# Query denominators in PSUM, another order of the query steps, and projections with the stationary tokens in two halves

## The chip, the core and the metric

The kernel runs on one core of a Trainium2 chip. A core has a matrix engine (TensorE, PE in the profile; its weight loads are listed apart as PEld), VectorE (DVE), ScalarE (ACT), GpSimd (POOL) and SyncE (SP), which issues the transfers. Each works through its own queue in order, and semaphores make one wait for another. SBUF is the working memory; PSUM, eight banks of 512 fp32 per partition, takes what TensorE writes. The metric is the device time of one execution in microseconds. The change is read as faster or slower where it differs from the time before by more than 2%.

## What is computed

Linear attention with a product of two small projections as feature map, and an MLP with a piecewise quadratic activation on its output.

```python
# batch, heads, sequence, head_dim = 4, 4, 1088, 32; r = 8; d_ff = 2048
def phi(x):
    a = np.einsum('rd,bhsd->bhsr', S1, x)
    b = np.einsum('rd,bhsd->bhsr', S2, x)
    return np.einsum('bhsi,bhsj->bhsij', a, b).reshape(*x.shape[:-1], r * r)
q_p, k_p = (phi(q), phi(k))
kv = np.einsum('bhsf,bhsd->bhfd', k_p, v)
z = np.sum(k_p, axis=2)
num = np.einsum('bhsf,bhfd->bhsd', q_p, kv)
den = np.einsum('bhsf,bhf->bhs', q_p, z)[..., None] + 1e-06
x = (num / den)            # then 4352 tokens of 4 * 32 = 128 values
h = x @ w_in               # 128 -> 2048
g = np.where(h >= 1, h, np.where(h <= -1, 0.0, (h + 1) ** 2 / 4))
out = g @ w_out            # 2048 -> 128
```

## The kernel before

A batch has nine tiles of 128 tokens, which are handled as three groups (`groups`) of three. For the keys of a batch, `features` multiplies each tile with the small matrix `s_sb` (the 128 tokens stationary, 64 columns moving; line 223), ScalarE copies one factor out of PSUM (line 227), and VectorE forms the 64 products per head (`kp`, line 229). `k_sums` then sums over all tokens in two PSUM banks (`kv`, line 255), and `projections` makes from the sums a third set of eight columns per head, so that a query tile, multiplied with the 96 columns of `proj`, also yields what its denominator needs.

For the queries of batches 1 to 3, a group goes through `q_steps_over`, four steps: `f` (`q_feat_over`: the projection `abc`, line 398; the copy `a_q`, 402; the products `ac`, 405; their sum, 406; 1e-6 added, 407; the reciprocal, 408; `a_q` times it, 409; the features `qp`, 411), `t` twice (`q_turn_over`: transposes `tp` and a copy), and `x` (`q_out`: the two matmuls of `xt`, line 436, each with 64 stationary columns and the output on one half of the partitions, and `place`, which writes the chunk's `x_hi` and `x_lo`). Batch 0 uses an older form of these steps, in `front` and in `q_steps`.

The MLP runs in 144 units: a chunk of 512 tokens (256 in the last) by 128 columns of d_ff. `up(u)` makes `h{u}` with three fp32r matmuls (high and low parts; lines 486 to 488), ScalarE and VectorE apply the activation (500, 501, 504, 505, or 507), GpSimd makes the low part `g_lo` (508), and `down` adds three matmuls into the chunk's `acc` (522 to 524), four units later. The first units of the first two chunks use whole fp32 (520) instead.

After every `up`, `advance` takes one step of the attention from a list: the string `FS` for batch 0, and `SS` for batches 1 to 3, where a digit and a letter name a query group and its step, and `k` is the next step of the next batch's keys. So the steps of all batches are done by about unit 62. The program is written in that order; a scheduler then fixes each engine's queue from it, so a step that is moved in the string can move other instructions too. Tiles come from pools, PSUM from one pool of eight banks.

Of the kernel before, what the change touches and what calls it, by code (L numbers as in the profile page):

```python
# [8 lines left out]
F32 = mybir.dt.float32  # L9
# [5 lines left out]
ALU = mybir.AluOpType  # L15
PSUM = bass.MemoryType.PSUM

P = 128
# [6 lines left out]
FIRST = 32  # L25
HI_ACT = (0.5, 0.35)
FS = "2t 2t 2n 2x s k k k k k k k"
SS = "0f k k 0t 0t 1f k 0x 1t k 1t 2f k 1x k 2t 2t k 2x"


def word_as_float(bits):
# [6 lines left out]
def tile_kernel(ctx: ExitStack, tc: tile.TileContext, qT, kT, v, S, w_in, w_out, outT):  # L38
    nc = tc.nc
    B, _, NTL, _ = qT.shape  # L40
    H, D, R = 4, 32, 8
# [8 lines left out]
    cst = ctx.enter_context(tc.tile_pool(name="cst", bufs=1))  # L50
    ld = ctx.enter_context(tc.tile_pool(name="ld", bufs=2))
    wk = ctx.enter_context(tc.tile_pool(name="wk", bufs=2))
# [4 lines left out]
    def bank(name):  # L57
        return ps.tile([P, 512], F32, tag="ps", name=name)
# [6 lines left out]
    for h in range(2):  # L65
# [5 lines left out]
                            axis=mybir.AxisListType.XY, op=ALU.add)  # L71
# [114 lines left out]
    s_sb = cst.tile([P, S.shape[1]], F32, name="s_sb")  # L186
# [27 lines left out]
    kv_sb = {}  # L214
    kv_part = {}


    def features(x_sb, grp, b, what, outs):

        n = len(grp)  # L220
        ab = bank(f"ab_{what}{b}_{grp[0]}")
        for i, t in enumerate(grp):
            nc.tensor.matmul(ab[:, i * 64 : (i + 1) * 64], lhsT=x_sb[:, t], rhs=s_sb, start=True, stop=True)
        a_sb = wk.tile([P, 3 * H, R], F32, tag="a_sb", name=f"a_{what}{b}_{grp[0]}", bufs=3)
        m = n * H
        abv = ab[:, : n * 64].rearrange("p (m c) -> p m c", c=2 * R)
        nc.scalar.copy(a_sb[:, :m], abv[:, :, :R])  # L227
        yield
        nc.vector.tensor_tensor(  # L229
            out=outs.rearrange("p t (h i j) -> p (t h) i j", h=H, i=R),  # L230
            in0=a_sb[:, :m].unsqueeze(3).broadcast_to([P, m, R, R]),
            in1=abv[:, :, R:].unsqueeze(2).broadcast_to([P, m, R, R]),
            op=ALU.mult,
        )
        yield
# [3 lines left out]
    def k_feat(b, g):  # L239
        if b not in batch:  # L240
            batch[b] = load_batch(b)
        if b not in kp_of:
            kp_of[b] = wk.tile([P, NTL, H * F], F32, tag="kw", name=f"kp{b}", bufs=1)
        grp = groups[g]
        yield from features(batch[b][0], grp, b, "k", kp_of[b][:, grp[0] : grp[-1] + 1])
# [52 lines left out]
    proj = {}  # L298
# [35 lines left out]
    def q_feat(b, g):  # L334
        grp = groups[g]
        qp_of[b, g] = wk.tile([P, 3, H * F], F32, tag="qp", name=f"qp{b}_{g}")
        yield from features(batch[b][2], grp, b, "q", qp_of[b, g][:, : len(grp)])
# [52 lines left out]
    def q_feat_over(b, g):  # L390

        grp = groups[g]
        n = len(grp)
        m = n * H
        q_sb = batch[b][2]
        abc = bank(f"abc{b}_{g}")
        for i, t in enumerate(grp):
            nc.tensor.matmul(abc[:, i * 96 : (i + 1) * 96], lhsT=q_sb[:, t], start=True, stop=True,  # L398
                             rhs=proj[b].rearrange("p h w r -> p (h w r)"))
        v3 = abc[:, : n * 96].rearrange("p (m c) -> p m c", c=3 * R)  # L400
        a_sb = wk.tile([P, 3 * H, R], F32, tag="a_sb", name=f"a_q{b}_{g}", bufs=3)
        nc.scalar.copy(a_sb[:, :m], v3[:, :, :R])
        ac = wk.tile([P, 3 * H, R], F32, tag="ac", name=f"ac{b}_{g}")
        den = wk.tile([P, 3 * H], F32, tag="dn", name=f"den{b}_{g}")
        nc.vector.tensor_tensor(out=ac[:, :m], in0=a_sb[:, :m], in1=v3[:, :, 2 * R :], op=ALU.mult)
        nc.vector.tensor_reduce(out=den[:, :m], in_=ac[:, :m], axis=mybir.AxisListType.X, op=ALU.add)
        nc.vector.tensor_scalar(out=den[:, :m], in0=den[:, :m], scalar1=1e-6, scalar2=None, op0=ALU.add)
        nc.vector.reciprocal(out=den[:, :m], in_=den[:, :m])
        nc.vector.tensor_tensor(out=a_sb[:, :m], in0=a_sb[:, :m], in1=den[:, :m].unsqueeze(2).broadcast_to([P, m, R]), op=ALU.mult)
        qp_of[b, g] = wk.tile([P, 3, H * F], F32, tag="qp", name=f"qp{b}_{g}")  # L410
        nc.vector.tensor_tensor(
            out=qp_of[b, g][:, :n].rearrange("p t (h i j) -> p (t h) i j", h=H, i=R),
            in0=a_sb[:, :m].unsqueeze(3).broadcast_to([P, m, R, R]),
            in1=v3[:, :, R : 2 * R].unsqueeze(2).broadcast_to([P, m, R, R]),
            op=ALU.mult,
        )
# [23 lines left out]
    def q_steps_over(b, g):  # L440
        q_feat_over(b, g)
        yield
        for p in range(2):
            q_turn_over(b, g, p)
            yield
        q_out(b, g)
        yield
# [128 lines left out]
    def merged(b, kb, seq):  # L576

        q = [(q_steps_over if b else q_steps)(b, g) for g in range(len(groups))]
        k = k_steps(kb) if kb < B else iter(())
        for e in seq.split():  # L580
            if e == "s":
                repeat_s2()
            elif e == "k":
                next(k, None)
                if kb >= B:
                    continue
            else:
                g = int(e[0])
                next(q[g])
                if e[1] == "x":  # L590
                    yield b * SEQ + min(SEQ, (g + 1) * 3 * P)
                    continue
            yield 0

    def steps():
        yield from merged(0, 1, FS)
        for b in range(1, B):
            yield from merged(b, b + 1, SS)

# [13 lines left out]
    for u in range(len(units)):  # L613
        c0, n, j = units[u]
        while todo and todo[0][0] <= j:
            _, make, c = todo.pop(0)
# [66 lines left out]
```

## Time and profile before

| | us |
|---|---|
| three runs | 287.23, 292.83, 371.11; median 292.83 |
| the profiled execution, device time | 287.16 |
| its span, first to last instruction | 285.3 |
| busy in the span: PE, DVE, ACT, POOL | 266.1, 218.5, 211.1, 190.6 |
| share of TensorE in the chain that ended last | 73% |

The rows have engine, line, operation, output and inputs, shape, count, then busy time and mean duration of one, and after the next bar how long the engine had idled before them and on whom. A row of the timeline starts with start and duration in us; neighbours of one kind are merged into one row with a count. Matmuls are pipelined, so the duration of one is longer than the time it keeps the array: what counts is the distance to the next start. An fp32 matmul leaves two records.

### The profile page before, as it was taken

The page shows a single profiled execution, that of the slowest core. Times are in us where ns is not written, and L with a number is a line of the kernel's source. Part 1 is how long each engine was busy: PE and PEld are TensorE (multiplying, and loading weights), DVE is VectorE, ACT ScalarE, POOL GpSimd, SP SyncE. Part 2 cuts the span into 40 slices and gives each one's busy share as a digit, 9 for nine tenths or more (in the row PEclk, how much of TensorE's full clock was granted, in tenths as well). Part 3 has the DMA queues.
Part 4 walks back from the last instruction along what each step waited for, and adds up shares of the span by engine and source line. Part 5 has one row for each costly group of instructions (what it writes and reads, how often), then busy time and mean ns, then how long its engine had stood idle before and what let it go on. Part 6 is the DMA issues. An engine that isn't in the chain of part 4 may idle for free.

```text
span 285.3 us, 4114 instructions
## 1 busy us (share of the span) xinstructions
PE 266.1 (93%) x1325; PEld 208.1 (73%) x1325; DVE 218.5 (77%) x387; ACT 211.1 (74%) x437; POOL 190.6 (67%) x171
## 2 busy tenths in 40 slices
PE   8876869999979999999995999999999999999994
PEld 5764747766749778778854777888888888888883
DVE  3547963969995789878875987788978778767774
ACT  2263845857557797957774677999999998989993
POOL 2071967067495565755573466799999989987892
PEclk9995659999999999999997999999999999999999
DMA  6999000220000100000000000010000000000001
GB/s 195 359 417 377 3 1 1 85 85 0 2 0 13 73 0 37 37 5 0 0 2 37 0 0 0 2 38 1 2 38 0 0 37 3 0 37 2 1 0 55
DMA packets 4772, 13.89 MB, mean 49 GB/s; under 512 B 528, under 2 KB 1296, under 8 KB 4752
## 3 DMA queue, kind: packets, MB, share of 16 engines
q1 hardware_dynamic: 4752, 13.64, 13.1%
q8 instruction: 10, 0.16, 0.2%
q14 instruction: 10, 0.08, 0.1%
HBM read 11.41 MB, written 2.23 MB: 48 GB/s over the span
## 4 chain that ended last, share of the span: by engine, by line
PE 73%; DVE 13%; ACT 5%; POOL 2%; DMA 2%; issue 2%; SPq 1%; DVEq 0%; ACTq 0%; POOLq 0%
PE h L486 10%; PE h L487 10%; PE h L488 10%; PE acc L524 9%; PE acc L522 8%; PE acc L523 8%; PE acc L520 5%; PE kv L255 4%; DMA v_sb<-in_v 2%; PE tp L425 2%; DVE s L505 2%; PE xt L436 2%; DVE g_hi L504 1%; PE abc L398 1%; ACT s L501 1%
## 5 line engine op out<-in xcount | busy, mean ns | idle before, releaser
L508 POOL TENSOR_TENSOR g_lo<-s,g_hi 128x512 fp32r<-128x512 f32 (+1 forms) x126 | 153.7, 1243 | 50.0 <-DVE s L505 23.7
L500 ACT ACTIVATE s<-h 128x512 f32<-128x512 f32 (+1 forms) x130 | 73.1, 573 | 28.8 <-PE h L488 27.0
L505 DVE SCALAR_TENSOR_TENSOR s<-h,s 128x512 f32<-128x512 f32 (+1 forms) x130 | 82.3, 653 | 7.3 <-ACT s L501 5.5
L501 ACT ACTIVATE s<-s 128x512 f32<-128x512 f32 (+1 forms) x130 | 76.7, 610 | 0.9
L504 DVE SCALAR_TENSOR_TENSOR g_hi<-h,s 128x512 fp32r<-128x512 f32 (+1 forms) x83 | 53.3, 648 | 27.3 <-ACT s L501 17.7
L486 PE MATMUL h<-x_hi,wi_hi 128*128 128x512 f32 (+1 forms) x144 | 61.0, 423 | 0.4 <-ACT x_hi L386 0.4
L487 PE MATMUL h<-x_lo,wi_hi 128*128 128x512 f32 (+1 forms) x144 | 56.0, 390 | 0.0
L488 PE MATMUL h<-x_hi,wi_lo 128*128 128x512 f32 (+1 forms) x144 | 55.6, 389 | 0.0
L524 PE MATMUL acc<-g_lo,wo_hi 128*128 128x512 f32 (+1 forms) x130 | 50.8, 396 | 1.8 <-POOL g_lo L508 1.1
L522 PE MATMUL acc<-g_hi,wo_lo 128*128 128x512 f32 (+1 forms) x130 | 50.4, 389 | 0.2 <-DVE g_hi L504 0.2
L523 PE MATMUL acc<-g_hi,wo_hi 128*128 128x512 f32 (+1 forms) x130 | 49.5, 381 | 0.0
L507 ACT CAST g_hi<-s 128x512 fp32r<-128x512 f32 (+1 forms) x47 | 28.3, 603 | 7.7 <-DVE s L505 7.5
L486 PEld LDWEIGHTS h<-x_hi,wi_hi 128*128 128x128 f32 x144 | 28.0, 195 | 7.9 <-issue 1.3
L488 PEld LDWEIGHTS h<-x_hi,wi_lo 128*128 128x128 f32 x144 | 27.7, 192 | 5.8
L487 PEld LDWEIGHTS h<-x_lo,wi_hi 128*128 128x128 f32 x144 | 28.0, 194 | 4.5 <-issue 0.2
L524 PEld LDWEIGHTS acc<-g_lo,wo_hi 128*128 128x128 f32 x130 | 24.4, 189 | 8.5 <-POOL g_lo L508 3.1
L522 PEld LDWEIGHTS acc<-g_hi,wo_lo 128*128 128x128 f32 x130 | 24.7, 190 | 6.1 <-issue 1.2
L130 POOL TENSOR_TENSOR loww<-loww,hcw 128x512 f32<-128x512 f32 x8 | 10.2, 1277 | 27.2 <-DVE hcw L105 26.8
L523 PEld LDWEIGHTS acc<-g_hi,wo_hi 128*128 128x128 f32 x130 | 24.5, 189 | 4.3
L255 PEld LDWEIGHTS kv<-v_sb,kp 128*128 128x128 f32 x108 | 14.4, 191 | 2.2 <-issue 1.0
L520 PE MATMUL acc<-s,wo 128*128 128x512 f32 x28 | 15.2, 664 | 0.8 <-DVE s L495 0.8
L229 DVE TENSOR_TENSOR kp<-a_k,ab_k 128x768 f32<-128x768 f32 x12 | 11.1, 943 | 4.4 <-ACT a_k L227 4.3
(96 smaller groups left out, 301.4 us busy)
## 6 DMA issues: line engine op xcount, KB each, us to landing
v_sb<-in_v SPq DMA_DIRECT2D x4, 594.0 KB, 8.5
raw_i<-in_w_in SPq DMA_DIRECT2D x4, 512.0 KB, 8.5
raw_o<-in_w_out SPq DMA_DIRECT2D x4, 512.0 KB, 7.6
outT<-o SPq DMA_DIRECT2D x8, 256.0 KB, 2.0
k_sb<-in_kT SPq DMA_DIRECT2D x3, 576.0 KB, 8.4
q_sb<-in_qT SPq DMA_DIRECT2D x3, 576.0 KB, 4.7
k_sb<-in_kT SPq DMA_DIRECT2D x3, 192.0 KB, 2.7
q_sb<-in_qT SPq DMA_DIRECT2D x1, 384.0 KB, 7.2
```

The source lines that it names most:

```text
L486: nc.tensor.matmul(h[:, :n], lhsT=wi_hi[:, fj], rhs=x_hi[:, :n], start=True, stop=False)
L487: nc.tensor.matmul(h[:, :n], lhsT=wi_hi[:, fj], rhs=x_lo[:, :n], start=False, stop=False)
L488: nc.tensor.matmul(h[:, :n], lhsT=wi_lo[:, fj], rhs=x_hi[:, :n], start=False, stop=True)
L500: nc.scalar.activation(s[:, :n], h[:, :n], AF.Relu, bias=0.5, scale=0.5)
L501: nc.scalar.activation(s[:, :n], s[:, :n], AF.Square)
L504: nc.vector.scalar_tensor_tensor(out=g_hi[:, :n], in0=h[:, :n], scalar=1.0, in1=s[:, :n], op0=ALU.max, op1=ALU.min)
L505: nc.vector.scalar_tensor_tensor(out=s[:, :n], in0=h[:, :n], scalar=1.0, in1=s[:, :n], op0=ALU.max, op1=ALU.min)
L508: (nc.vector if u >= len(units) - 4 else nc.gpsimd).tensor_tensor(out=g_lo[:, :n], in0=s[:, :n], in1=g_hi[:, :n].bitcast(F32), op=ALU.subt ...
L520: nc.tensor.matmul(acc[:, :n], lhsT=wo_32[:, fj], rhs=g_hi[:, :n], start=(j == 0), stop=False)
L522: nc.tensor.matmul(acc[:, :n], lhsT=wo_lo[:, fj], rhs=g_hi[:, :n], start=(j == 0), stop=False)
L523: nc.tensor.matmul(acc[:, :n], lhsT=wo_hi[:, fj], rhs=g_hi[:, :n], start=False, stop=False)
L524: nc.tensor.matmul(acc[:, :n], lhsT=wo_hi[:, fj], rhs=g_lo[:, :n], start=False, stop=(j == NJ - 1))
```

## The change

It has three parts. In `q_feat_over` the denominator is kept in twelve unused columns of the group's own PSUM bank `abc`; the products go into one of two fixed tiles `terms`, which hold 1e-6 as a ninth value, so the sum over nine replaces the sum over eight and the separate addition. The key projections and the query projections of batches 1 to 3 load the 128 stationary tokens as two halves of 64, each with its output on one half of the partitions: two matmuls in place of one. And the string `SS` is another.

```diff
-SS = "0f k k 0t 0t 1f k 0x 1t k 1t 2f k 1x k 2t 2t k 2x"
+SS = "0f k 1f k 0t k 0t k 2f 0x k 1t 1t k 1x k 2t 2t 2x"
...
+    terms = [cst.tile([P, 3 * H, R + 1], F32, name=f"terms{i}") for i in range(2)]
+    for t in terms:
+        nc.gpsimd.memset(t[:, :, R:], 1e-6)
...
         for i, t in enumerate(grp):
-            nc.tensor.matmul(ab[:, i * 64 : (i + 1) * 64], lhsT=x_sb[:, t], rhs=s_sb, start=True, stop=True)
+            for c in (slice(0, 64), slice(64, P)) if b else (slice(0, P),):
+                nc.tensor.matmul(ab[c, i * 64 : (i + 1) * 64], lhsT=x_sb[:, t, c], rhs=s_sb, start=True, stop=True)
...
         for i, t in enumerate(grp):
-            nc.tensor.matmul(abc[:, i * 96 : (i + 1) * 96], lhsT=q_sb[:, t], start=True, stop=True,
-                             rhs=proj[b].rearrange("p h w r -> p (h w r)"))
+            for c in (slice(0, 64), slice(64, P)):
+                nc.tensor.matmul(abc[c, i * 96 : (i + 1) * 96], lhsT=q_sb[:, t, c], start=True, stop=True,
+                                 rhs=proj[b].rearrange("p h w r -> p (h w r)"))
...
-        ac = wk.tile([P, 3 * H, R], F32, tag="ac", name=f"ac{b}_{g}")
-        den = wk.tile([P, 3 * H], F32, tag="dn", name=f"den{b}_{g}")
-        nc.vector.tensor_tensor(out=ac[:, :m], in0=a_sb[:, :m], in1=v3[:, :, 2 * R :], op=ALU.mult)
-        nc.vector.tensor_reduce(out=den[:, :m], in_=ac[:, :m], axis=mybir.AxisListType.X, op=ALU.add)
-        nc.vector.tensor_scalar(out=den[:, :m], in0=den[:, :m], scalar1=1e-6, scalar2=None, op0=ALU.add)
-        nc.vector.reciprocal(out=den[:, :m], in_=den[:, :m])
-        nc.vector.tensor_tensor(out=a_sb[:, :m], in0=a_sb[:, :m], in1=den[:, :m].unsqueeze(2).broadcast_to([P, m, R]), op=ALU.mult)
+        ac = terms[g % 2]
+        den = abc[:, 3 * 96 : 3 * 96 + m]
+        nc.vector.tensor_tensor(out=ac[:, :m, :R], in0=a_sb[:, :m], in1=v3[:, :, 2 * R :], op=ALU.mult)
+        nc.vector.tensor_reduce(out=den, in_=ac[:, :m], axis=mybir.AxisListType.X, op=ALU.add)
+        nc.vector.reciprocal(out=den, in_=den)
+        nc.vector.tensor_tensor(out=a_sb[:, :m], in0=a_sb[:, :m], in1=den.unsqueeze(2).broadcast_to([P, m, R]), op=ALU.mult)
```

What the string and the scheduler make of it is seen in the engines' queues. In the rows below a name is followed by its batch and group (`xt2_1` is batch 2, group 1; `h45` is the hidden tile of unit 45) and a running number; the lines of the changed kernel are five higher. First TensorE's queue where the output of batch 2, group 1 is made, before:

```order
L436 MATMUL xt2_1_1376<-qpT2_1_1261,kv_d2_1019 64x384 x2
L486 MATMUL h45_1386<-x_hi1024_418,wi_hi_127 128x512
L487 MATMUL h45_1386<-x_lo1024_419,wi_hi_127 128x512
L488 MATMUL h45_1386<-x_hi1024_418,wi_lo_128 128x512
L255 MATMUL kv3_0_1282<-v_sb3_1095,kp3_1099 128x66
```

And now:

```order
L441 MATMUL xt2_1_1431<-qpT2_1_1366,kv_d2_1000 64x384
L491 MATMUL h46_1441<-x_hi1024_422,wi_hi_127 128x512
L492 MATMUL h46_1441<-x_lo1024_423,wi_hi_127 128x512
L493 MATMUL h46_1441<-x_hi1024_422,wi_lo_128 128x512
L314 MATMUL w3_1455<-zm3_1453,s2_rep_136 128x16 x2
L527 MATMUL acc1024_1236<-g_hi42_1359,wo_lo_130 128x512
L528 MATMUL acc1024_1236<-g_hi42_1359,wo_hi_129 128x512
L441 MATMUL xt2_1_1431<-qpT2_1_1366,kv_d2_1000 64x384
```

The two matmuls of one `xt` stood next to each other and now have seven others between them. The same holds for xt1_2, xt3_1 and xt3_2; xt2_2 was parted already.

Next TensorE's queue at the start of batch 3's queries, before, from the projection to the first transposes:

```order
L398 MATMUL abc3_0_1512<-proj3_1468,q_sb3_1094 128x96 x3
L486 MATMUL h51_1530<-x_hi1536_927,wi_hi_127 128x512
L524 MATMUL acc1024_1203<-g_lo46_1416,wo_hi_129 128x512
L487 MATMUL h51_1530<-x_lo1536_928,wi_hi_127 128x512
L488 MATMUL h51_1530<-x_hi1536_927,wi_lo_128 128x512
L522 MATMUL acc1024_1203<-g_hi47_1436,wo_lo_130 128x512
L523 MATMUL acc1024_1203<-g_hi47_1436,wo_hi_129 128x512
L524 MATMUL acc1024_1203<-g_lo47_1437,wo_hi_129 128x512
L425 MATMUL tp3_0_0_1543<-ident_73,qp3_0_1525 128x128 x3
```

And now, from behind unit 51:

```order
L404 MATMUL abc3_0_1543<-proj3_1458,q_sb3_1116 64x96 x5
L441 MATMUL xt2_2_1519<-qpT2_2_1478,kv_d2_1000 64x320
L404 MATMUL abc3_0_1543<-proj3_1458,q_sb3_1116 64x96
L529 MATMUL acc1024_1236<-g_lo46_1447,wo_hi_129 128x512
...
L404 MATMUL abc3_1_1573<-proj3_1458,q_sb3_1116 64x96 x6
L527 MATMUL acc1024_1236<-g_hi47_1471,wo_lo_130 128x512
L528 MATMUL acc1024_1236<-g_hi47_1471,wo_hi_129 128x512
L529 MATMUL acc1024_1236<-g_lo47_1472,wo_hi_129 128x512
L491 MATMUL h52_1594<-x_hi1536_973,wi_hi_127 128x512
L492 MATMUL h52_1594<-x_lo1536_974,wi_hi_127 128x512
L493 MATMUL h52_1594<-x_hi1536_973,wi_lo_128 128x512
L430 MATMUL tp3_0_0_1607<-ident_73,qp3_0_1556 128x128 x3
```

The projection of group 1 and unit 52 now stand ahead of the transposes of group 0, and half of xt2_2 stands inside the projection of group 0.

At the same place VectorE's queue was, from the products of group 0 to its features:

```order
L405 TENSOR_TENSOR ac3_0_1518<-a_q3_0_1516,abc3_0_1512 128x96
L387 TENSOR_TENSOR x_lo3072_1494<-xt2_2_1488,x_hi3072_1493 128x192
L505 SCALAR_TENSOR_TENSOR s50_1504<-h50_1500,s50_1504 128x512
L406 TENSOR_REDUCE den3_0_1519<-ac3_0_1518 128x12
L407 TENSOR_SCALAR den3_0_1519<-den3_0_1519 128x12
L505 SCALAR_TENSOR_TENSOR s51_1534<-h51_1530,s51_1534 128x512
L408 RECIPROCAL den3_0_1519<-den3_0_1519 128x12
L409 TENSOR_TENSOR a_q3_0_1516<-a_q3_0_1516,den3_0_1519 128x96
L411 TENSOR_TENSOR qp3_0_1525<-a_q3_0_1516,abc3_0_1512 128x768
```

And now:

```order
L411 TENSOR_TENSOR terms0_132<-a_q3_0_1550,abc3_0_1543 128x12x8
L392 TENSOR_TENSOR x_lo3072_1525<-xt2_2_1519,x_hi3072_1524 128x192
L510 SCALAR_TENSOR_TENSOR s50_1535<-h50_1531,s50_1535 128x512
L412 TENSOR_REDUCE abc3_0_1543<-terms0_132 128x12
L411 TENSOR_TENSOR terms1_133<-a_q3_1_1580,abc3_1_1573 128x12x8
L510 SCALAR_TENSOR_TENSOR s51_1565<-h51_1561,s51_1565 128x512
L413 RECIPROCAL abc3_0_1543<-abc3_0_1543 128x12
L412 TENSOR_REDUCE abc3_1_1573<-terms1_133 128x12
L414 TENSOR_TENSOR a_q3_0_1550<-a_q3_0_1550,abc3_0_1543 128x96
L413 RECIPROCAL abc3_1_1573<-abc3_1_1573 128x12
L416 TENSOR_TENSOR qp3_0_1556<-a_q3_0_1550,abc3_0_1543 128x768
```

The addition is gone, and three operations of group 1 have come in ahead of the features of group 0.

## The prediction

> **What bounds the kernel now.** I read the busy time by stretch first (columns: stretch in us, its length, busy time of PE, PE weight loads, DVE, ACT and POOL with instruction counts, granted clock, DMA share, GB/s), then who TensorE waited for between 60 and 180 us.
>
> ```profile
> 64.00:90.00 26.00, 23.32 (x126) 17.18 (x125) 22.39 (x40) 17.25 (x37) 17.49 (x14) 1.00 0.00 1
> 90.00:143.00 53.00, 52.87 (x293) 42.57 (x293) 45.20 (x84) 39.87 (x83) 31.10 (x27) 1.00 0.07 22
> 143.00:157.00 14.00, 10.34 (x43) 7.07 (x41) 8.92 (x17) 8.29 (x18) 7.51 (x6) 0.88 0.05 20
> 157.00:176.00 19.00, 19.00 (x95) 13.67 (x94) 16.33 (x30) 13.33 (x27) 10.41 (x8) 1.00 0.00 0
> ...
> PE tp L425 <- DVE qp L411: 4.2, 2, 3.7
> PE acc L524 <- POOL g_lo L508: 1.1, 1, 1.1
> PE acc L520 <- DVE s L495: 0.8, 2, 0.6
> ```
>
> The change acts between 45 and 176 us, where the steps of batches 1 to 3 are woven into the MLP units. There TensorE is the bound, with two holes: 26.00 - 23.32 = 2.7 us idle between 64 and 90, where VectorE is nearly full (22.39 of 26), and 14.00 - 10.34 = 3.7 us idle between 143 and 157. Between 90 and 143 and between 157 and 176 PE is idle for 0.1 us in all. So VectorE time is worth something in the holes only, and TensorE time is worth its full length outside them. What lies behind 176 us is not touched and keeps its length.
>
> **Part 1, the denominator.** VectorE's groups in the nine query groups of batches 1 to 3:
>
> ```profile
> L405 DVE TENSOR_TENSOR ac<-a_q,abc 128x96 f32<-128x96 f32 x9 | 2.2, 247 | 0.0
> L407 DVE TENSOR_SCALAR den<-den 128x12 f32<-128x12 f32 x9 | 6.2, 688 | 0.1
> L409 DVE TENSOR_TENSOR a_q<-a_q,den 128x96 f32<-128x96 f32 x9 | 6.6, 737 | 0.2
> ```
>
> L407 handles 12 elements in 688 ns and L409 takes 737 ns for the size that L405 does in 247. The timeline of one group tells why (VectorE, then GpSimd at the same time):
>
> ```profile
> 131.62 0.80 DVE L407 TENSOR_SCALAR den<-den 128x12 f32<-128x12 f32 x1
> ...
> 132.72 1.19 DVE L409 TENSOR_TENSOR a_q<-a_q,den 128x96 f32<-128x96 f32 x1
> ...
> 131.09 2.70 POOL L508 TENSOR_TENSOR g_lo<-s,g_hi 128x512 fp32r<-128x512 f32 x2 [1.03 <-DVE s L505]
> ```
>
> GpSimd runs two g_lo back to back, so the first ends at 131.09 + 1.35 = 132.44 and the second at 133.79. L407 ends at 132.42 and L409 at 133.91: both sit until a GpSimd operation is over. Both have all operands in SBUF; L405, with one operand in PSUM, does not sit. The change removes L407 (its 1e-6 becomes a ninth term of the sum, set once by two small memsets ahead of everything on GpSimd, hidden behind the first loads) and gives L409 a PSUM operand, as L405 has. VectorE gains 9 x 0.69 = 6.2 us and 9 x (0.737 - 0.247) = 4.4 us, 10.6 us in all. The sum over nine instead of eight terms and a reciprocal that reads and writes PSUM I take at their old price. On the path this gives nothing of itself outside the holes, where PE's own work covers it; what it gives in them is in part 4.
>
> **Part 2, 128 stationary tokens as two halves.** This doubles the matmuls of nine key groups and nine query groups. The trace has one place that uses 64 stationary columns with the output on half of the partitions: xt (L436). First a pair of halves, as PE and as weight loads, then a single half:
>
> ```profile
> 78.48 0.40 PE L523 MATMUL acc<-g_hi,wo_hi 128*128 128x512 f32 x1
> 78.81 0.87 PE L436 MATMUL xt<-qpT,kv_d 128*64 128x384 f32 x4
> 79.60 0.50 PE L486 MATMUL h<-x_hi,wi_hi 128*128 128x512 f32 x1
> 79.94 0.39 PE L487 MATMUL h<-x_lo,wi_hi 128*128 128x512 f32 x1
> ...
> 78.80 0.20 PEld L436 LDWEIGHTS xt<-qpT,kv_d 128*64 128x64 f32 x4 [0.37 <-DVE den L406]
> 79.60 0.19 PEld L486 LDWEIGHTS h<-x_hi,wi_hi 128*128 128x128 f32 x1 [0.60 <-DVE kp L229]
> ...
> 143.63 0.40 PE L523 MATMUL acc<-g_hi,wo_hi 128*128 128x512 f32 x1
> 143.96 0.75 PE L436 MATMUL xt<-qpT,kv_d 128*64 128x320 f32 x2
> 144.65 0.51 PE L524 MATMUL acc<-g_lo,wo_hi 128*128 128x512 f32 x1
> 144.99 0.39 PE L522 MATMUL acc<-g_hi,wo_lo 128*128 128x512 f32 x1
> ```
>
> Each fp32 matmul makes two records, and 512 columns of the MLP follow each other every 0.23 us (79.94 against the next, and so all through). The pair then holds the array from 78.48 + 0.23 = 78.71 to 79.94 - 0.23 = 79.71: 1.00 us for two halves of 384 columns. The single half of 320 columns holds it from 143.86 to 144.76: 0.90 us. If a second half costs nothing, 2 x 384 s + o = 1.00 and 2 x 320 s + o = 0.90, so s is about 0.8 ns for a column and pass and o about 0.38 us. That fits: both halves run at once, and o is what the change of shape costs, since no weight load is made ahead on either side of it (the loads sat idle for 0.37 and 0.60 us, and the next full-width load begins with its own matmul, at 79.60).
> The Trainium skill, "TensorEngine Tiling (Array Packing)", Key Properties, says that tiles load weights and multiply in parallel, but that changing the tiling mode drains the array; by that rule the trace agrees with both halves of the sentence, and o of 0.38 us is the drain's price here. By its section Theoretical Speedup, up to 2x for 64 columns, a group would take half of its time; that is a rival below.
>
> What the groups cost now, a key group and a query group between MLP matmuls:
>
> ```profile
> 65.54 0.39 PE L488 MATMUL h<-x_hi,wi_lo 128*128 128x512 f32 x1
> 65.77 0.78 PE L223 MATMUL ab_k<-s_sb,k_sb 128*128 128x64 f32 x6
> 66.36 0.48 PE L486 MATMUL h<-x_hi,wi_hi 128*128 128x512 f32 x1
> 66.67 0.39 PE L487 MATMUL h<-x_lo,wi_hi 128*128 128x512 f32 x1
> ...
> 75.28 0.39 PE L488 MATMUL h<-x_hi,wi_lo 128*128 128x512 f32 x1
> 75.50 0.80 PE L398 MATMUL abc<-proj,q_sb 128*128 128x96 f32 x6
> 76.09 0.48 PE L486 MATMUL h<-x_hi,wi_hi 128*128 128x512 f32 x1
> 76.41 0.39 PE L487 MATMUL h<-x_lo,wi_hi 128*128 128x512 f32 x1
> ```
>
> By the same reckoning a key group holds the array from 65.77 to 66.44 and a query group from 75.51 to 76.18: 0.67 us each, six records at 0.112 us, the same for 64 and for 96 moving columns, so the full-width weight load sets it. In halves the four loads of xt start within 0.20 us less one load (0.134 us by the group row below), so passes follow every 0.06 us or less.
>
> ```profile
> L436 PEld LDWEIGHTS xt<-qpT,kv_d 128*64 128x64 f32 x36 | 2.0, 134 | 3.1 <-issue 1.1 <-DVE den L406 1.1 <-DVE s L505 0.7
> ```
>
> Six passes with both halves at once: a key group 0.38 + 6 x 0.057 = 0.72 us, a query group 0.38 + 6 x 96 x 0.8 ns = 0.84 us. So the halving gives nothing and costs 9 x 0.05 + 9 x 0.17 = 2.0 us. Ends: without o, 0.34 and 0.46 us, which is -4.9 us; with the halves one after the other, 9 x 0.39 + 9 x 0.63 = +9.2 us. I take the price of the xt rows, the only ones of this shape.
>
> **Part 3, what the order does to xt.** The two halves of an xt stand together in eight of nine groups before (only xt2_2 is split). In the new order xt1_2, xt2_1, xt2_2, xt3_1 and xt3_2 have other work between their halves. A half by itself costs as much as the pair: +1.0 us for xt2_1 and xt3_1 each and +0.9 for xt3_2. The second halves of xt1_2 and xt2_2 stand inside the halved matmuls of a query group and share its change of shape: 2 x 320 x 0.8 = 0.51 us less a little overlap, 0.45. So xt1_2 costs +0.45, and xt2_2, which paid 0.9 twice, -0.45. Sum +2.9 us. Parts 2 and 3 make 4.9 us more of TensorE work; some 0.3 of it (five halved groups before 90 us) falls into the first hole and is free there.
>
> **Part 4, the holes.** The second hole, with VectorE beside it:
>
> ```profile
> 149.10 0.40 PE L524 MATMUL acc<-g_lo,wo_hi 128*128 128x512 f32 x1
> 153.15 0.90 PE L425 MATMUL tp<-ident,qp 128*128 128x128 f32 x3 [3.66 <-DVE qp L411]
> 154.28 0.63 PE L487 MATMUL h<-x_lo,wi_hi 128*128 128x512 f32 x1
> 155.63 0.60 PE L522 MATMUL acc<-g_hi,wo_lo 128*128 128x512 f32 x1
> ...
> 148.97 0.68 DVE L505 SCALAR_TENSOR_TENSOR s<-h,s 128x512 f32<-128x512 f32 x1
> 149.84 1.25 DVE L407 TENSOR_SCALAR den<-den 128x12 f32<-128x12 f32 x1
> 151.00 0.68 DVE L505 SCALAR_TENSOR_TENSOR s<-h,s 128x512 f32<-128x512 f32 x1
> 152.15 0.95 DVE L411 TENSOR_TENSOR qp<-a_q,abc 128x768 f32<-128x768 f32 x1
> ```
>
> TensorE waits for qp3_0, held up by the 1.25 us of L407. In the new order VectorE puts the product, sum and reciprocal of group 1 ahead of qp3_0 (3 x about 0.24 = 0.7 us) and loses 1.25, so qp3_0 comes only some 0.3 us earlier, near 152.8. But TensorE now has h52 (three times 0.23) and group 1's projection (0.84) ahead of tp3_0_0, 1.5 us of work that it did behind the hole. With its own halved groups it arrives near 150.6 and sits for some 2.3 us instead of 3.7: -1.4. Behind the hole the clock was halved: from 153.15 to 155.63 PE did two transposed groups of 0.33 and one h of 0.69 us in 2.48 us, 1.1 us lost. A shorter hole may not trip it: -0.8.
> In the first hole VectorE had 22.39 of 26 us, of which L407 and L409 give back about 2.3 us in its two query groups. The third group is pulled in (1.9 us of work), and GpSimd's weight conversion moves behind four more g_lo, which takes 2.6 us off the g_lo that PE waited 1.1 us for; it still ends ahead of the unit that reads it. Of 2.7 us idle I let 2.5 go. The keys that now come later and the other moved steps land in stretches where PE has work queued, so I cost them at nothing; if that cover fails, the next thing late is acc<-g_hi behind a late VectorE.
>
> **Sum.** +4.9 - 0.3 - 2.5 - 1.4 - 0.8 = -0.1 us on the profiled execution's own 287.16 us: 287.0 us. That execution is next to the lowest of the runs shown (287.23); the median of the three, 292.83, is 2% above it, and I predict against the lower two, which agree.
>
> **Rivals.**
> Halves without the price of the change of shape (the 2x of the skill's page): -4.9 in place of +2.0, so 280.1 us. For it: two halves of xt cost what one does. Against it: every xt row carries the 0.38. Chance 0.14.
> The holes close altogether: -2.7 - 3.7 - 1.1 with +4.6 gives 284.3. For it: 10.6 us of VectorE time against 6.4 us of holes. Against it: the new order brings three operations ahead of qp3_0. Chance 0.17.
> The holes stay as they are: 287.2 + 4.6 = 291.8. For it: group 2 pulled into the full first stretch. Chance 0.18.
> Slower: inside a group the halves run one after the other, since six small matmuls with the same moving tokens queue in order; that is part 2's +9.2 in place of +2.0, 294.2 us. It decides from about +6 us on TensorE. Against it: the loads of xt. Chance 0.08.
> My own forecast 0.43.
>
> Range 280.5 to 292.5: it takes in all but part of the first and the last rival. About 2% is what a measurement of this kernel can tell from no change, 281.4 and 292.9 us here. Faster takes the first rival and a quarter of the second: 0.18. Slower takes the last and a little of the third: 0.11. Same: 0.71.
>
> **What would show it.** Right: a key group in halves holding the array for about 0.72 us and a query group 0.84, with weight loads idle ahead of and behind each; xt1_2, xt2_1, xt3_1 and xt3_2 as single halves of 0.9 to 1.0 us; a_q<-a_q at about 250 ns; a hole of about 2.3 us near 150 without a lower clock behind it; PE idle in the 64 to 90 stretch under 0.5 us. Wrong: halved groups at 0.35 us, or over 1.0; a new idle time of PE behind VectorE between units 16 and 30.

## The result, and the profile after

| | before | after |
|---|---|---|
| median of 20 runs | 287.64 us | 284.51 us |
| range (two runs of before near 371 us left out) | 285.67 to 292.83 | 280.83 to 285.79 |
| ratio, 95% interval | | 0.9861 [0.9827, 0.9895] |
| the profiled execution, device time | 287.16 us | 284.93 us |
| its span | 285.3 us | 283.1 us |

The changed kernel is 1.4% faster, which lies within the 2% that count as no change, though outside the measurement's own uncertainty. The forecast was 287.0 us, that is no gain; 3.1 us were gained between the medians and 2.2 us between the two profiled spans.

The times of one kernel spread by some 3%, and its mean granted clock varies with them (0.941 to 0.988 for before); in the traces the half clock comes in pieces of 3.4 us, two to six of them in the first 45 us. The ratios leave out runs more than 1.5% above the lowest, so for e1 to e4 below, where before ranged from 282.1 to 291.47 us, they rest on its 8 lowest of 29 runs and come out higher than the medians would. Parts of a few tenths of a microsecond are therefore not compared by device time here, but in the traces, one execution of each kernel, by the time from the first matmul of unit 8 to the first matmul of unit 64, called the stretch below. It holds nearly all query work of batches 1 to 3, and in the traces of before and after all that lies outside it differs by 0.6 us. The stretch took 128.57 us before and 125.81 us after: 2.76 us less.

The page's totals of after (engine, busy time, share of the span, instructions) show the two sides of the change: VectorE lost 8.4 us of its 218.5, and TensorE gained 3.5 us on its 266.1.

```profile
PE 269.6 (95%) x1433; PEld 204.0 (72%) x1433; DVE 210.1 (74%) x378; ACT 210.8 (74%) x437; POOL 191.0 (67%) x173
```

The busy time by stretch of after, in the columns of the prediction:

```profile
64.00:90.00 26.00, 25.96 (x184) 19.01 (x183) 21.87 (x45) 18.37 (x38) 18.02 (x15) 1.00 0.08 24
90.00:143.00 53.00, 53.00 (x312) 39.43 (x311) 40.64 (x74) 39.99 (x83) 33.27 (x27) 1.00 0.03 11
143.00:157.00 14.00, 12.45 (x81) 8.10 (x80) 11.14 (x26) 9.44 (x21) 7.12 (x6) 1.00 0.05 20
157.00:176.00 19.00, 19.00 (x82) 12.49 (x82) 12.46 (x23) 14.03 (x28) 11.08 (x10) 1.00 0.00 0
```

And the whole list of TensorE's waits between 60 and 180 us (total, times, longest):

```profile
PE tp L430 <- DVE qp L416: 1.6, 1, 1.6
```

The first hole (64 to 90) is gone: 0.04 us idle instead of 2.7, although VectorE is still busy for 21.87 of the 26 us. The second is down from 3.7 to 1.6 us, and the granted clock behind it reads 1.00 where it was 0.88. One wait is left where before had four kinds (the three of the prediction, and 0.2 us for g_hi).

VectorE's groups in the nine query groups of batches 1 to 3 are all near 250 ns now, and the line that took 688 ns is gone:

```profile
L412 DVE TENSOR_REDUCE abc<-terms 128x12 f32<-128x108 f32 x9 | 2.4, 262 | 0.1
L414 DVE TENSOR_TENSOR a_q<-a_q,abc 128x96 f32<-128x96 f32 x9 | 2.2, 248 | 0.1
L411 DVE TENSOR_TENSOR terms<-a_q,abc 128x96 f32<-128x96 f32 x9 | 2.2, 246 | 0.0
...
L413 DVE RECIPROCAL abc<-abc 128x12 f32<-128x12 f32 x9 | 2.1, 236 | 0.1
```

What a halved key group and a halved query group hold of the array is seen in TensorE's timeline of after, which has one of each between MLP matmuls:

```profile
65.61 0.40 PE L493 MATMUL h<-x_hi,wi_lo 128*128 128x512 f32 x1
65.94 0.57 PE L228 MATMUL ab_k<-s_sb,k_sb 128*64 128x64 f32 x12
66.44 0.50 PE L491 MATMUL h<-x_hi,wi_hi 128*128 128x512 f32 x1
66.78 0.39 PE L492 MATMUL h<-x_lo,wi_hi 128*128 128x512 f32 x1
67.01 0.40 PE L493 MATMUL h<-x_hi,wi_lo 128*128 128x512 f32 x1
67.33 0.72 PE L404 MATMUL abc<-proj,q_sb 128*64 128x96 f32 x12
67.98 0.50 PE L527 MATMUL acc<-g_hi,wo_lo 128*128 128x512 f32 x1
68.32 0.39 PE L528 MATMUL acc<-g_hi,wo_hi 128*128 128x512 f32 x1
```

By the reckoning of the prediction the key group holds it from 65.84 to 66.55, 0.71 us, and the query group from 67.24 to 68.09, 0.85 us. Both were 0.67 us at full width. Twelve matmuls stand where six stood, but the two halves of a pass start 6 to 7 ns apart in the trace and run at the same time. What eats the gain is the change of shape at both ends, 0.85 - 6 x 0.082 = 0.36 us for the query group, whose passes follow each other every 0.082 us in the trace, and 0.70 - 6 x 0.058 = 0.35 us for a key group.

Three places of TensorE's timeline after show what became of `xt`: a single half in the open, a half inside a query group's projection, and the second hole.

```profile
133.92 0.40 PE L529 MATMUL acc<-g_lo,wo_hi 128*128 128x512 f32 x1
134.25 0.86 PE L441 MATMUL xt<-qpT,kv_d 128*64 128x384 f32 x2
135.04 0.50 PE L491 MATMUL h<-x_hi,wi_hi 128*128 128x512 f32 x1
135.38 0.39 PE L492 MATMUL h<-x_lo,wi_hi 128*128 128x512 f32 x1
...
144.64 0.40 PE L493 MATMUL h<-x_hi,wi_lo 128*128 128x512 f32 x1
144.97 0.63 PE L404 MATMUL abc<-proj,q_sb 128*64 128x96 f32 x9
145.35 0.43 PE L441 MATMUL xt<-qpT,kv_d 128*64 128x320 f32 x1
145.43 0.25 PE L404 MATMUL abc<-proj,q_sb 128*64 128x96 f32 x1
145.62 0.43 PE L441 MATMUL xt<-qpT,kv_d 128*64 128x320 f32 x1
145.89 0.33 PE L404 MATMUL abc<-proj,q_sb 128*64 128x96 f32 x2
146.15 0.50 PE L529 MATMUL acc<-g_lo,wo_hi 128*128 128x512 f32 x1
146.49 0.39 PE L491 MATMUL h<-x_hi,wi_hi 128*128 128x512 f32 x1
...
149.18 0.40 PE L493 MATMUL h<-x_hi,wi_lo 128*128 128x512 f32 x1
151.13 0.55 PE L430 MATMUL tp<-ident,qp 128*128 128x128 f32 x3 [1.55 <-DVE qp L416]
```

The single half of 384 columns holds the array from 134.15 to 135.15, 1.00 us, as much as a pair of halves did. The half of 320 columns inside the projection makes that group last from 144.87 to 146.26, 1.39 us instead of 0.85: 0.54 us. The last two rows are what is left of the second hole.

### The profile page after: what moved, and what is told of

It is laid out like the page before. It is cut to its first block, busy times and chain, and to the rows that moved or that the text cites. A ratio compares the mean times of both kernels' runs of the same rounds, so it can differ in the third digit from the quotient of the medians.

```text
span 283.1 us, 4325 instructions
## 1 busy us (share of the span) xinstructions
PE 269.6 (95%) x1433; PEld 204.0 (72%) x1433; DVE 210.1 (74%) x378; ACT 210.8 (74%) x437; POOL 191.0 (67%) x173
## 4 chain that ended last, share of the span: by engine, by line
PE 84%; DVE 6%; POOL 2%; ACT 2%; DMA 2%; issue 1%; SPq 1%; DVEq 0%; POOLq 0%; ACTq 0%
PE h L491 12%; PE h L492 11%; PE h L493 11%; PE acc L529 10%; PE acc L527 10%; PE acc L528 10%; PE acc L525 5%; PE kv L260 4%; PE xt L441 4%; DMA v_sb<-in_v 2%; PE tp L430 2%; PE abc L404 2%; PE ab_k L228 2%; PE kv L277 1%; POOL loww L130 1%; DVE g_lo L513 1%
## 5 line engine op out<-in xcount | busy, mean ns | idle before, releaser
L491 PE MATMUL h<-x_hi,wi_hi 128*128 128x512 f32 (+1 forms) x144 | 60.1, 418 | 0.4 <-ACT x_hi L391 0.4
L529 PE MATMUL acc<-g_lo,wo_hi 128*128 128x512 f32 (+1 forms) x130 | 51.8, 399 | 0.8 <-DVE g_lo L513 0.6
```

The costliest lines, as they stand in the source:

```text
L491: nc.tensor.matmul(h[:, :n], lhsT=wi_hi[:, fj], rhs=x_hi[:, :n], start=True, stop=False)
L529: nc.tensor.matmul(acc[:, :n], lhsT=wo_hi[:, fj], rhs=g_lo[:, :n], start=False, stop=(j == NJ - 1))
```

## The experiments

A word on how they are read. Waits are summed over the stretch by the distance between neighbouring starts of full-width matmuls, less the usual distance (0.23 us for 512 columns, 0.43 for whole fp32, 0.11 for the small ones), where the two differ by more than 0.15 us; this takes in what half clock adds to a distance. Where the record of a matmul is missing from the trace, its usual distance is taken off too. The sum is 8.7 us before and 1.9 us after. How well the traces repeat is seen where two kernels have the same work: units 12 to 28 take 37.51 us in before and in e10, 34.65 in e2 and in e9, 33.96 in e6 and in e8. The stretch of e8, e9 and e10 takes in three more matmuls of `acc` than that of the others (143 against 140), which is 0.7 us. None of the ten kernels leaves out a part of the computation.

| kernel | median, us | ratio to before, 95% | stretch, us | waits in it, us |
|---|---|---|---|---|
| before | 287.64 | | 128.57 | 8.7 |
| after | 284.51 | 0.9861 [0.9827, 0.9895] | 125.81 | 1.9 |
| e1 denominator alone | 285.31 | 0.9994 [0.9921, 1.0066] | 127.98 | 7.4 |
| e2 order alone | 285.75 | 1.0064 [1.0018, 1.0109] | 126.68 | 2.3 |
| e3 halves alone | 290.55 | 1.0194 [1.0117, 1.0271] | 131.89 | 9.6 |
| e4 after, full width | 283.20 | 0.9930 [0.9878, 0.9983] | 124.68 | 1.7 |
| e5 after, xt in pairs | 280.79 | 0.9753 [0.9711, 0.9796] | 121.42 | 1.4 |
| e6 both of e4 and e5 | 277.71 | 0.9674 [0.9634, 0.9715] | 120.17 | 1.6 |
| e7 after, denominator in SBUF | 283.58 | 0.9838 [0.9792, 0.9884] | 125.75 | 2.2 |
| e8 e6 and a pause for batch 3 | 275.97 | 0.9601 [0.9562, 0.9639] | 119.36 | 0.2 |
| e9 e8, old denominator | 277.44 | 0.9639 [0.9592, 0.9685] | 119.91 | 0.5 |
| e10 before, xt in pairs, a pause | 281.96 | 0.9790 [0.9745, 0.9835] | 124.56 | 4.9 |

Measured beside them, before had medians of 288.1 (e1 to e4), 287.99 (e5 to e8) and 288.65 us (e9, e10). All are judged by the stretch first.

**e1, the denominator alone.** The new denominator in the order and the widths of before; both projections are put back to full width, of which the cut shows the second.

```diff
-SS = "0f k 1f k 0t k 0t k 2f 0x k 1t 1t k 1x k 2t 2t 2x"
+SS = "0f k k 0t 0t 1f k 0x 1t k 1t 2f k 1x k 2t 2t k 2x"
...
-            for c in (slice(0, 64), slice(64, P)):
+            for c in (slice(0, P),):
```

> Kernel before with the denominators in PSUM alone (old order, full-width projections). Theory: the two idle stretches of TensorE (2.7 us between 64 and 90, 3.7 us near 150, and the 1.1 us lost to the halved clock behind it) come from VectorE sitting out GpSimd operations in den<-den and a_q<-a_q,den; so this edit alone takes 3 to 5 us off (some 283 to 284 where before has 287.6), less 0.9 us for the one xt (batch 3, group 2) that its queue parts, and a_q<-a_q falls from 737 to about 250 ns. Rival, that the new order closes them: this edit alone gives less than 1.5 us, and TensorE still idles over 3 us near 150.

The stretch got 0.6 us shorter: 1.3 us less of waits, and an xt of batch 3 that this kernel's order parts as well (0.9 us). TensorE's waits between 60 and 180 us:

```profile
PE tp L430 <- DVE qp L416: 3.3, 2, 3.1
PE acc L529 <- POOL g_lo L513: 1.0, 1, 1.0
```

The busy time by stretch:

```profile
64.00:90.00 26.00, 24.75 (x140) 19.18 (x138) 22.46 (x42) 17.91 (x36) 19.27 (x17) 1.00 0.05 15
143.00:157.00 14.00, 10.92 (x45) 8.14 (x45) 7.98 (x18) 7.23 (x16) 4.92 (x5) 0.76 0.05 19
```

The long wait is 3.1 us where it was 3.7, the wait for g_lo is as it was, and the half clock behind the second hole is there again, for longer. The first hole is halved (1.25 us idle of 26 instead of 2.7). By the distances between starts the first hole fell from 3.5 to 1.9 us and the second from 3.8 to 3.2, while the half clock cost 2.2 us instead of 1.1. So VectorE's time alone closes neither.

**e2, the order alone.** Only the string is new; denominator and widths are those of before.

```diff
-SS = "0f k k 0t 0t 1f k 0x 1t k 1t 2f k 1x k 2t 2t k 2x"
+SS = "0f k 1f k 0t k 0t k 2f 0x k 1t 1t k 1x k 2t 2t 2x"
```

> Kernel before with the new string of steps alone. Its queue parts six of nine xt (before: one): five more single halves at 0.9 to 1.0 us, +4.8 us. Theory (VectorE's waits make the idle stretches): they shrink by 2 us at most, so +2.5 to +5 us on before. Rival (the order closes them): they fall by 5 us or more, so the time is that of before or lower.

TensorE's waits between 60 and 180 us, then the busy time by stretch, then the two groups of VectorE that the new denominator would shorten:

```profile
PE tp L427 <- DVE qp L413: 1.6, 1, 1.6
PE tp L427 <- DVE s L507: 0.2, 1, 0.2
```

```profile
64.00:90.00 26.00, 25.79 (x147) 20.08 (x147) 23.35 (x47) 18.31 (x38) 17.49 (x15) 1.00 0.07 24
...
143.00:157.00 14.00, 12.45 (x63) 9.29 (x63) 11.63 (x29) 9.61 (x21) 7.28 (x6) 1.00 0.05 20
```

```profile
L409 DVE TENSOR_SCALAR den<-den 128x12 f32<-128x12 f32 x9 | 3.9, 430 | 0.1
L411 DVE TENSOR_TENSOR a_q<-a_q,den 128x96 f32<-128x96 f32 x9 | 2.8, 311 | 0.1
```

Both holes are where the changed kernel has them, with the old denominator and with VectorE at 23.35 of 26 us in the first: 6.4 us of waits are gone. The stretch is only 1.9 us shorter because six of the nine xt now stand in two pieces. The order closes most of the holes; what is left of them is 1.7 us by the starts in the second and 0.5 in the first.

**e3, the halves alone.** Both projections in halves, in before.

```diff
+            for c in (slice(0, 64), slice(64, P)) if b else (slice(0, P),):
+                nc.tensor.matmul(ab[c, i * 64 : (i + 1) * 64], lhsT=x_sb[:, t, c], rhs=s_sb, start=True, stop=True)
...
+            for c in (slice(0, 64), slice(64, P)):
+                nc.tensor.matmul(abc[c, i * 96 : (i + 1) * 96], lhsT=q_sb[:, t, c], start=True, stop=True,
+                                 rhs=proj[b].rearrange("p h w r -> p (h w r)"))
```

> Kernel before with the projections in two halves alone. Theory: each key group 0.70 in place of 0.67 us, each query group 0.85 in place of 0.67, nine of each, +1.9 us, and +0.9 for the xt of batch 3, group 2, which its queue parts; some of it hidden in the idle stretches: +1.5 to +2.8 us. Rival (halves shorten the wait of ScalarE and VectorE for the projections, or run at half the time): -1 us or less.

The stretch is 3.3 us longer, half a microsecond beyond the expected span. By what the groups hold of the array in before and after, the halved ones make 1.8 us of it (six key groups at 0.03, nine query groups at 0.18), an xt3_2 that this kernel's order parts as well 0.9, and a new wait for qp near 114 us 1.5; the half of xt2_2 that moved into a projection gives 0.35 back, and other waits are shorter. TensorE's waits between 60 and 180 us:

```profile
PE tp L427 <- DVE qp L413: 5.7, 3, 3.8
PE acc L526 <- POOL g_lo L510: 0.9, 1, 0.9
PE acc L522 <- DVE s L497: 0.6, 1, 0.6
```

**e4, after at full width.** Both projections are put back; the cut shows the second.

```diff
-            for c in (slice(0, 64), slice(64, P)):
+            for c in (slice(0, P),):
```

> The changed kernel with full-width projections, the rest as it is; the same five xt are parted. Theory: -1.9 us for the groups, and +0.9 since the second halves of xt1_2 and xt2_2 no longer share the change of shape with a projection: -1 us on the changed kernel (283.5 where it has 284.5). Rival (the halves bring the gain): +2 us or more.

The stretch is 1.13 us shorter than that of after, as expected. The halves are a loss in the changed kernel too. e4 and e2 differ in the denominator alone, and their stretches by 2.0 us: 0.6 us of it is waits, and some 1.1 us is a sixth xt, xt3_0, which e2's queue parts and e4's does not. So in the new order the denominator is worth more than in e1, but mostly by what the scheduler makes of it.

**e5, after with the two halves of an xt together.** The first half also waits for the copy that the second one needs, so that the scheduler can't put other work between them.

```diff
-        nc_copy(qpT[:, p, : n * P], tp[:, : n * P])
+        copied[b, g] = nc_copy(qpT[:, p, : n * P], tp[:, : n * P])
...
+            half = nc.tensor.matmul(xt[p * 64 : (p + 1) * 64, :m], lhsT=kv_part[b][:, p],
+                                    rhs=qpT_of[b, g][:, p, :m], start=True, stop=True)
+            if p == 0:
+                after(half, copied[b, g])
```

> The changed kernel, with the first half of each xt made to wait for the copy that the second half needs, so that all nine xt stand as pairs in TensorE's queue. Theory (a half by itself costs as much as a pair): from unit 8 to unit 64 it takes 2 to 3 us less than the changed kernel's 125.8 us, so 123 to 124. Rival (the parted halves fill time that was idle anyway, or waiting for the copy makes TensorE wait): 125.5 or more.

The stretch is 4.4 us shorter than that of after, where 2 to 3 were expected. The expectation left out that xt2_2, which before parted already, becomes a pair too, and that a half inside a query group costs 0.54 us. From the rows above: three single halves more than pairs need (1.0, 1.0 and 0.9) and two halves inside projections (0.54 each) are 4.0 us, and the waits fell by 0.5.

**e6, both.** e4 and e5 in one kernel.

> Both undone: full-width projections and all xt as pairs, the new order and the denominators in PSUM kept. Theory: the halving's 1.9 us and the parted xt's 2.2 us are TensorE work and add up, so unit 8 to unit 64 takes about 121.8 us (125.8 before that), and about 280.5 us in all where the changed kernel has 284.5. Rival (TensorE's idle time grows by what its work loses): 124 or more from unit 8 to unit 64.

120.17 us, 1.6 us better than expected, and 5.6 us less than after. Next to e5 the halves cost 1.25 us, next to e4 the parted xt 4.5.

**e7, after with the denominator in SBUF.** The ninth term stays, so line 407's addition stays away; only the place of the denominator goes back.

```diff
-        den = abc[:, 3 * 96 : 3 * 96 + m]
+        den = wk.tile([P, 3 * H], F32, tag="dn", name=f"den{b}_{g}")[:, :m]
```

> The changed kernel with the denominator in an SBUF tile again; the ninth term stays, so the separate addition is still gone. Theory: a_q<-a_q,den has all operands in SBUF, sits out GpSimd operations again and takes 500 ns or more on the mean where it has 248; since the new order leaves TensorE little idle time, the stretch from unit 8 to unit 64 grows by 0 to 1 us only. Rival (the PSUM operand is what closes the idle stretches): +2 us or more, with TensorE waiting for qp over 3 us near 150.

VectorE's group of this kernel, then TensorE's one wait:

```profile
L414 DVE TENSOR_TENSOR a_q<-a_q,den 128x96 f32<-128x96 f32 x9 | 4.9, 548 | 0.1
```

```profile
PE tp L430 <- DVE qp L416: 1.7, 1, 1.7
```

The operation takes 548 ns instead of 248, as all operands are in SBUF again, and the stretch does not notice (125.75 us against 125.81). PSUM as the denominator's place gains VectorE 9 x 0.30 = 2.7 us that nobody waits for.

**e8, what the other runs point to.** e6, and a string of its own for batch 3, with two units that bring no step between the features of groups 0 and 1 and the first transposes. There are no keys left to prepare then, so the `k` steps of `SS` pass without a unit.

```diff
+LS = "0f 1f - - 0t 0t 2f 0x 1t 1t 1x 2t 2t 2x"
...
+            elif e == "-":
+                pass
...
-            yield from merged(b, b + 1, SS)
+            yield from merged(b, b + 1, SS if b + 1 < B else LS)
```

> As the kernel with full-width projections and paired xt, and batch 3 gets two units without a step of its own ahead of its first transposes. Theory: the 1.6 us that TensorE still waits for qp3_0 near 150 has two units of other work in front of it and goes: some 1.5 us less, 120.3 us from unit 8 to unit 64 and 279 in all. Rival: the wait comes back at a later transpose and the time is that of the kernel without the two units.

Busy time by stretch of this kernel:

```profile
64.00:90.00 26.00, 25.97 (x146) 20.53 (x145) 23.33 (x46) 19.31 (x40) 18.00 (x16) 1.00 0.08 24
90.00:143.00 53.00, 53.00 (x290) 41.99 (x290) 40.94 (x79) 41.16 (x88) 34.41 (x27) 1.00 0.03 11
143.00:157.00 14.00, 14.00 (x71) 10.86 (x70) 12.85 (x28) 12.07 (x23) 10.26 (x8) 1.00 0.05 19
```

No wait is listed any more, and TensorE is busy in every microsecond of the last two rows. 275.97 us, 4.0% less than before, is the fastest of all kernels here. Next to e6 the stretch is 0.8 us shorter where 1.5 was expected: the waits fell by 1.4 us, and the three more matmuls of `acc` take 0.7 back.

**e9, e8 with the old denominator.**

> The mended kernel (new order, full-width projections, paired xt, two units without a step in batch 3) with the old denominators: a separate addition and all in SBUF. Theory (the order closes the idle stretches, VectorE has time to spare behind it): at most 1 us more than the mended kernel's 119.4 us from unit 8 to unit 64, although VectorE is busy some 5 to 10 us longer. Rival (the denominators are worth their VectorE time): 122 or more.

VectorE's groups of the old denominator in this kernel:

```profile
L410 DVE TENSOR_SCALAR den<-den 128x12 f32<-128x12 f32 x9 | 5.5, 616 | 0.0
L412 DVE TENSOR_TENSOR a_q<-a_q,den 128x96 f32<-128x96 f32 x9 | 4.3, 473 | 0.1
```

The stretch is 0.55 us longer than e8's, and the medians are 1.5 us apart, with intervals of the ratios that overlap. So in a kernel without holes, and with xt in pairs, the new denominator, 5.5 + 9 x (0.473 - 0.244) = 7.6 us of VectorE's time here (e8's a_q<-a_q takes 244 ns), is worth about half a microsecond.

**e10, before with a pause.** The old order, widths and denominator; xt in pairs as in e5, and the pause of e8 in the old order.

```diff
+LS = "0f - - 0t 0t 1f 0x 1t 1t 2f 1x 2t 2t 2x"
```

> The kernel before with paired xt and two units without a step ahead of batch 3's first transposes, nothing else: old order in batches 1 and 2, old denominators. Theory: the idle stretch near 150 (3.8 us between two matmuls) and the half clock behind it (1.1 us) go, the parted xt of batch 2, group 2 too (0.8 us): 122.5 to 123.5 us from unit 8 to unit 64 where before has 128.6; the stretch between units 12 and 28 stays at 37.5. Rival (the wait for qp3_0 moves along): 126 or more.

TensorE's waits between 60 and 180 us (the first two rows), then the busy time by stretch:

```profile
PE tp L430 <- DVE qp L414: 1.2, 2, 0.7
PE acc L531 <- POOL g_lo L515: 1.1, 1, 1.1
```

```profile
64.00:90.00 26.00, 23.36 (x127) 17.36 (x126) 22.57 (x41) 16.48 (x34) 17.21 (x16) 1.00 0.02 3
143.00:157.00 14.00, 14.00 (x71) 10.73 (x70) 13.23 (x27) 11.65 (x24) 9.99 (x8) 1.00 0.05 20
```

The second hole is closed entirely (14.00 of 14), the first is exactly as before (2.6 us idle; units 12 to 28 take 37.51 us in both). The stretch is 4.0 us shorter, 1 us short of the expectation: between 157 and 176 us a new wait of 0.7 us for qp came up, and the three more matmuls of `acc` are 0.7 us. Two empty units and the pairing of one xt gained more than the whole change did.

## Why the prediction was right or wrong

The time lay in the range and on the side that was called likeliest, but the terms of the sum were not all of the right size. That the change counts as none is owed to the margin more than to the sum: 2.8 us were gained in the stretch where the sum had 0.1, and 2% are 5.7 us. (287.16 - 0.1 is 287.1; the 287.0 is a slip of rounding.) In the stretch the terms compare like this:

| term | forecast, us | measured, us |
|---|---|---|
| halves | +2.0 | +1.8 by the groups' rows; undoing them wins 1.1 (e4) or 1.25 (e6 against e5) |
| parted xt, beside the halves | +2.9 | +3.1 by the rows |
| first hole | -2.5 | -3.3 |
| second hole | -1.4 | -2.1 |
| half clock behind it | -0.8 | -1.1 |
| elsewhere: halved groups hidden; a wait near 124 us | -0.3 | -0.3 |
| sum | -0.1 | -1.9 by the rows, against -2.76 in the stretch |

So 0.9 us of the gain is in none of the rows, and what it is was not found.

**Part 1 was right.** VectorE's operations came to the predicted length (248 ns against 247), and what they gave was worth little by itself: 0.6 us of the stretch in e1. The nine groups lost 10.3 us, near the 10.6 of the forecast, but VectorE's total only 8.4. The reason that the prediction gave can be said more exactly now. By the Trainium skill, "SBUF — State Buffer", Who interferes with whom, a VectorE operation with two SBUF inputs and a GpSimd operation that reads SBUF keep each other out for the whole of an instruction. The trace agrees: with the denominator in SBUF the same operation took 548 ns, in PSUM 248. Who waits is decided by who starts first: in before six of the nine a_q<-a_q,den began while a g_lo was running, and all six ended 114 to 117 ns after it; the other three, of which one began 14 ns ahead of a g_lo, took 242 to 259 ns. The addition, with one input from SBUF, waited in the same way: all nine began under a GpSimd operation and ended 27 to 33 ns after it. So the price hangs on the order as well: with the old denominator in the new order (e2) the two operations that took 688 and 737 ns in before took 430 and 311 ns, and only one of the nine a_q<-a_q,den met a running GpSimd operation. The 10.6 us were a property of the old order as much as of the tile.

**Part 2 had the mechanism, and nearly the sizes.** 0.71 and 0.85 us for a group were forecast as 0.72 and 0.84; both halves run at once, and the change of shape costs 0.36 us. The rival at twice the speed falls, and so does the one with halves one after the other. By the Trainium skill, "TensorEngine Tiling (Array Packing)", Key Properties, a change of mode drains the array; the rows fit that, with 0.36 us beyond the passes of a query group. It takes more than the halves save: six full-width passes last 0.67 us, six halved ones 6 x 0.082 = 0.49, or 6 x 0.058 = 0.35 in a key group. In the stretch the halves cost less than the groups' own rows say (1.8 us, as in e3). With e4 the difference is known: its two xt halves inside projections pay 0.89 us each instead of 0.54, so 0.7 us of the loss comes back. Between e5 and e6 no xt is parted, 0.2 us is in the waits, and some 0.35 us stays unexplained.

**Part 3 was right**, to 0.2 us: the xt that were named as parted are the ones, single halves cost 1.00 and 0.90 us, and e5 shows what they cost together.

**Part 4 is the step that failed**, in size and in what it credited. "Of 2.7 us idle I let 2.5 go" takes a hole for the idle time in TensorE's rows. But a matmul's record lasts 0.39 us, and the next one usually starts after 0.23, so every wait is 0.16 us longer than the idle time shown. The five waits of the first hole add up to 3.5 us by the distance between starts, and nearly all of it went.

In the second hole two things were off. VectorE was to deliver qp3_0 0.3 us earlier (its own figures, 1.25 less 0.7, give 0.55); in fact, from the first matmul of abc3_0 to the transposes that wait for its features it took 153.15 - 146.93 = 6.22 us before and 151.13 - 144.97 = 6.16 us after. The start of the projection before, and the product of group 0 before and after:

```profile
146.93 0.91 PE L398 MATMUL abc<-proj,q_sb 128*128 128x96 f32 x6
...
148.54 0.24 DVE L405 TENSOR_TENSOR ac<-a_q,abc 128x96 f32<-128x96 f32 x1
...
147.60 0.24 DVE L411 TENSOR_TENSOR terms<-a_q,abc 128x96 f32<-128x96 f32 x1
```

From the product to the transposes it was 4.61 us before and 3.53 after, so VectorE did gain 1.1 us, with the three operations of group 1 in between. It was lost ahead of the product, which began 1.61 us after the projection's start before and 2.63 us after it in the changed kernel: the projection, with the half of xt2_2 inside it, lasts 1.25 us there instead of 0.90, and ScalarE casts xt and runs an activation before it copies a_q. And TensorE had not 1.5 but 2.0 us more work in that time: the half of xt2_2 inside the projection (0.54 us), which Part 3 had booked as a cost, stands ahead of the wait and is covered by it. The hole shrank by 4.05 - 1.95 = 2.1 us, all of it TensorE's own work moved ahead of the wait. e2 has the same 1.95 us without the new denominator, and e4, which has it, 1.70.

So the rival "the holes close altogether" (284.3 us) named the size better than the forecast did, for a reason that fell: it argued from VectorE's 10.6 us against 6.4 us of holes. With them alone (e1) 7.4 of 8.7 us of waits stay, 1.1 us of them because the half clock lasted longer. What closed most of the holes was the order, which puts other work of TensorE between a projection and the transposes that follow it. "The holes stay" falls with the same rows.

**The sum.** The change gained little because most of what it won is given back: the waits are 6.8 us shorter, nearly all of it by the order (6.4 us in e2), and the parting of xt, which the same order brings, and the halves make TensorE's own work longer, 4.9 us by their rows, of which the stretch shows 6.8 - 2.8 = 4.0. e6 keeps the shorter waits and drops both costs, and e8 takes the rest of the second hole.

What stays open: why the first hole closes by just this order. The five waits are gone in e2, but for some tenths of a microsecond, and all stand in e10; which of the moved steps closes them was not tried apart.

## What to carry to other kernels

A wait of the bounding engine is closed by its own work that does not depend on the late engine, put ahead of the wait; in the second hole making the late engine faster (e1) moved it by half a microsecond where reordering (e2) moved it by two. When steps are reordered, look at what the order pulls apart: two matmuls that share a change of the array's shape cost as much apart, each, as they do together. And size a hole by the distance between starts and not by idle time, and count work that moves into it as free.

## What the runs showed of the hardware

- A matmul with half of the columns costs the array as much alone as with its partner: 1.00 us for one half of 384 columns and for both, 0.90 us for 320 columns.
- Among other matmuls of the same shape that half costs 0.54 us, since it shares their change of shape.
- Changing the shape there and back costs 0.36 us for a query group (0.85 - 6 x 0.082), and 0.35 us for a key group (0.70 - 6 x 0.058).
- A VectorE operation with both inputs in SBUF that began while a g_lo ran on GpSimd ended 114 to 117 ns after it (six of nine in before); the three that did not took 242 to 259 ns.
- After the hole of 3.66 us in before, and after that of 3.08 us in e1, the clock was halved for 3.4 and 6.8 us. After 1.55 us in after and in e2 it was not.
